# A gated mix of two spectral filters: another division of PSUM in the loop of steps, and another order of products and gate sums

## The chip, the cores and the metric

The kernel runs on one core of one Trainium2 chip. The metric is the time of one execution on the device in microseconds (us); each time shown is the median of several runs.

## The reference

Two filters are applied to the same input `x` (2048 × 1024, bf16), each a two-dimensional real Fourier transform, a pointwise product with complex weights and the inverse transform; a gate of one number per row mixes them.

```python
def ref(x, w_r, w_i):
    X = rfft2(x.astype(float32))
    return irfft2(X * (w_r + 1j * w_i), s=(S, D)).astype(bfloat16)

g = sigmoid((x * gate_w).sum(-1, keepdims=True))
return g * ref(x, A_w_r, A_w_i) + (1 - g) * ref(x, B_w_r, B_w_i)
```

The gate's sum over a row is taken from the spectrum too, since only the forward transform of the columns is at hand when it is needed.

## The kernel before, in words

Both filters share one forward transform, and the two inverse transforms are mixed before the last stage. All transforms are matrix products with constant matrices.

- Stage 1 (`stage1`, L387) transforms along one part of the rows; `fold3` (L442, VectorE) adds and subtracts halves of the result. The parts for the first four row frequencies go to the small tiles EO and VD.
- Then comes the **loop of steps**, 16 of them, one for each pair of row frequencies in each half of the columns. `SEQ` gives the order: pairs (half 0, p = 0, 1, 2), (half 1, p = 0), (half 0, p = 3 to 7), (half 1, p = 1 to 7). In this text "pair i" is entry i of SEQ; pairs 0 to 8 without pair 3 are the first pass over half 0, and pair 8 is its last. `step(i)` issues stage 4 of pair i (`stage4`, L481; evicted from PSUM by ScalarE, L485, into one of six buffers X), the swap of real and imaginary rows of X into a buffer XS (`swap`, two DMAs, L290; on POOL's queue for i up to 7, on SP's after), and stage 2 of pair i + 2 (`stage2`, L455 and L464; evicted by ScalarE, L470, into one of three buffers CS). Behind each step come the gate's matmuls (`gate_spectrum`, L511, eight for each row frequency), whose 32 columns are evicted once (L660, into GSB) in step 10, and the products of that step.
- A **product** (`product`, L499, VectorE) multiplies X (for `sw` = 0) or XS (`sw` = 1) of a pair by the weights of both filters: (i, 0) and (i, 1) in ORDER. The entries with two more numbers are products of one half only. The weights are loaded by SP's queue in the order of p; pair 8 (p = 7) needs the last of them.
- The **groups** (`group`, L606) are the first part of the inverse transform: 16 matmuls each into a slot of two banks, evicted by ScalarE (L616) or VectorE (L614). Groups 0 to 15 need the products of half 0, groups 16 to 31 those of half 1. `spare` hands out the slots in turn: three of them until step 15 is issued, then four.
- The **gate**: `row_sums` (three instructions of VectorE, L526 to L530) makes the sums from GSB. `zsum` (L553, 32 matmuls, and a sigmoid by ScalarE, L556, into VD) and `gate_mask` (L562) make the mask for one half of the rows; `rbgen` (L593) multiplies the constant matrix by the mask, which gives 16 row blocks RB.
- Stages 6 (L735) and 7 (L760) are the rest of the inverse transform, row block by row block, with their evictions and sums (L745, L767, L743, L807, L771, and L812 on POOL) and the stores.

PSUM has eight banks. In the loop, stage 2 uses banks 0 and 1 in each step (pair 1 uses 4 and 5, pairs 13 and 15 use 6 and 7), stage 4 the banks 2 and 3 or 4 and 5 in turn, and the gate's columns lie in bank 6, after the gate weights in bank 7.

What orders the work: each engine runs its instructions in the order in which the program adds them. An instruction names keys that it reads and writes (a bank, a buffer), and the program adds semaphore waits for the earlier instructions on these keys. Nothing is reordered. Several reads and writes of VD share one key, so that a fold into VD also waits for the matmuls that read VD before.

Of the kernel before, what the change touches and what calls it, by code (L numbers as in the profile page):

```python
# [5 lines left out]
ACT = mybir.ActivationFunctionType  # L6
# [228 lines left out]
def bass_gated_mix__spectral_gfnet__spectral_gfnet__prompt_kernel(nc, A_x, A_w_r, A_w_i, B_x, B_w_r, B_w_i, gate_w, out):  # L235
# [22 lines left out]
    VD = sb("VD", 1024)  # L258
# [24 lines left out]
    P = Prog()  # L283
# [142 lines left out]
    def fblock(cmb, j, t):  # L426
        if cmb in (1, 2):
            return sl(FT, cmb * 4096 + j * 2048 + t * 128, [(1, 128)])
        if t < 4:
            return sl((EO, VD)[t // 2], cmb // 3 * 512 + j * 256 + t % 2 * 128, [(1, 128)])  # L430
        return sl(FT, cmb * 4096 + j * 2048 + (t - 4) * 128, [(1, 128)])

    def ekeys(i, cs, s):
        return [("E", i, cs, s)] + ["VD"] * (i == 1)
# [10 lines left out]

    def stage2(i, css=(0, 1), ab=(0, 1)):
        hf, p = SEQ[i]
        b0 = 4 if i == 1 else 6 if i in (13, 15) else 0
        if 0 in ab:
            for cs in css:  # L450
                for t in (2 * p, 2 * p + 1):
                    for j in range(2):
                        o = ps((b0 + t % 2) * 512 + cs * 256 + 32, [(96, 2), (64, 2), (1, 32)])
                        rh = sl(F2, 256 + 512 * cs + 256 * j + hf * 128, [(1, 128)])
                        P.add("pe", lambda e, o=o, cs=cs, j=j, t=t, rh=rh: e.matmul(o, fblock(1 + cs, j, t), rh, start=(j == 0), stop=(j == 1)),  # L455
                              r=[("F1", cs, j), "F2"], w=[bank(b0 + t % 2)])
        if 1 in ab:
            for cs in css:
                for t in (2 * p, 2 * p + 1):
                    for w in range(2):  # L460
                        v = 1 - w if cs else w
                        o = ps((b0 + t % 2) * 512 + cs * 256 + 64 * v, [(224 - 128 * v, 2), (1, 32)])
                        rh = sl(F2, 1280 * cs + w * 128 + hf * 64, [(1, 64)])
                        op = P.add("pe", lambda e, o=o, cs=cs, t=t, w=w, rh=rh: e.matmul(o, fblock(3 * cs, w, t), rh, start=True, stop=True),  # L464
                                   r=ekeys(p, cs, w) + ["F2"], w=[bank(b0 + t % 2)])
        if css == (0,) or ab == (0,):
            return
        dst, src = sl(XF, CSo(i), [(1, 1024)]), ps(b0 * 512, [(128, 8), (1, 32), (32, 4)])
        kw = dict(r=[bank(b0), bank(b0 + 1)], w=[("CS", i % 3)], after=last1)
        P.add("act", lambda e: e.activation(dst, src, ACT.Copy), **kw)  # L470
        return op

    def stage4(i):
        b0 = 2 + 2 * (i % 2 if i < STEP5 else 0)
        parts = [(1, 0, 1), (0, 1, 1)] if SEQ[i][1] == 0 else [(0, 0, 2)]
        for pm in range(2):
            for kind, q, n in parts:
                for m in range(2):
                    o = ps((b0 + pm) * 512 + q * 256, [(1, n * 256)])
                    rh = sl(XF, CSo(i) + 512 * q + 256 * m, [(512, n), (1, 256)])  # L480
                    P.add("pe", lambda e, o=o, kind=kind, pm=pm, m=m, rh=rh: e.matmul(o, sl(CK, fbo(kind, pm, m), [(1, 128)]), rh,  # L481
                                                                                      start=(m == 0), stop=(m == 1)),
                          r=[("CS", i % 3), "CK"], w=[bank(b0 + pm)])
        dst = sl(XF, Xo(i), [(1, 1024)])
        P.add("act", lambda e: e.activation(dst, ps(b0 * 512, [(256, 2), (512, 2), (1, 256)]), ACT.Copy), r=[bank(b0), bank(b0 + 1)],  # L485
              w=[("X", i % NX)], after=last1)

    def swap(i):
        eng = ("pool", "sp")[i > 7]
        for ri in range(2):  # L490
            dma(eng, f"xs{i}", sl(MM, XSo(i), [(1, 1024)], p0=1 - ri, np_=64, pstep=2), sl(XF, Xo(i), [(1, 1024)], p0=ri, np_=64, pstep=2),
                r=[("X", i % NX)], **({"a": [("XS", i % NX)]} if ri else {"w": [("XS", i % NX)]}), after=last1)
# [15 lines left out]

    def gate_spectrum(t):
        for m in range(8):  # L510
            P.add("pe", lambda e, m=m: e.matmul(ps(6 * 512 + 2 * t, [(1, 2)]), fblock(m // 2, m % 2, t), sl(CK, GWo + 2 * m, [(1, 2)]),  # L511
                                                start=(m == 0), stop=(m == 7)), r=["GW2"] + ([("F1", m // 4, m % 2)] if m // 2 in (1, 2) else ekeys(t // 2, m // 4, m % 2)), w=[bank(6)])

    def star_column(b):
        for o, n, kind, pm, off in ((2, 15, 0, 0, 3), (3, 15, 0, 1, 3), (0, 1, 1, 0, 1), (1, 1, 1, 1, 1)):
# [32 lines left out]

    GMo = lambda r: (XF, 7168 + r * 256) if r < 8 else (MM, 4096 + (r - 8) * 256)

    def zsum(u, hf):
        for n in range(32):
            P.add("pe", lambda e, n=n: e.matmul(ps(u * 1024 + 32 * n, [(1, 32)]), sl(AB, n, [(0, 128)]), sl(CL, MKo + 32 * hf, [(1, 32)]),  # L553
                                                start=True, stop=True),
                  r=["AB", "CV"], w=[bank(2 * u + n // 16)])
        P.add("act", lambda e: e.activation(sl(VD, 0, [(1, 1024)]), ps(u * 1024, [(1, 32), (32, 32)]), ACT.Sigmoid, scale=SM[:, 0:1]),  # L556
              r=[bank(2 * u), bank(2 * u + 1), "SM"], w=["VD"])

    def gate_mask(hf):
        t, o = GMo(8 * hf)  # L560
        for h in range(2):
            P.add("dve", lambda e, h=h: e.tensor_scalar(  # L562
                out=sl(t, o + h * 32, [(64, 32), (1, 32)]), in0=sl(VD, 0, [(32, 32), (1, 32)]),
                scalar1=SM[:, 1 + h:2 + h], scalar2=None, op0=ALU.mult),
                r=["VD", "SM"], w=[("GM", hf, h), ("XS" if hf else "X", 4), ("XS" if hf else "X", 5)])


    def col0(u, sw):
# [51 lines left out]
    for cs in range(2):  # L620
        for i in range(2):
            fold3(i, (cs,))
        for ab in range(2):
            for i in range(2):
                stage2(i, (cs,), (ab,))
            if cs == ab == 0:
                gate_weights(7)
    for i in range(2, 6):
        fold3(i)
    load("CL", CL, 576, CL.shape[1] - 576, cst["CL"].ap()[:, 576:], w=["CL", "GR", "GRr"])  # L630
# [4 lines left out]
    def step(i):  # L635
# [5 lines left out]
        if i == 15:  # L641
            dma("sp", "U5", sl(FT, U5o, [(2048, 8), (1, 1024)]).bitcast(u16), cst["U5"].ap().rearrange("p (a b) -> p a b", a=8), w=["U5"], after=[last2])


    ORDER = (((0, 0),), ((1, 0),), ((2, 0),), ((3, 0),), ((0, 1), (4, 0)), ((1, 1), (2, 1), (5, 0)), ((3, 1), (6, 0)), ((4, 1), (7, 0)),
             ((5, 1), (8, 0, 0, 1)), ((6, 1), (7, 1)), ((8, 1, 0, 1), (8, 0, 1, 1), (8, 1, 1, 1), (9, 0)), ((9, 1), (10, 0)), ((10, 1), (11, 0)), ((11, 1), (12, 0)))

    def products(i):
        for a in ORDER[i]:
# [3 lines left out]
    for i in range(STEP5):  # L653
        step(i)
        for _ in range(2 if i == 0 else 1):
            if gt < 16:
                gate_spectrum(gt)
                gt += 1
        if i == 10:
            P.add("act", lambda e: e.activation(GSB[:], ps(6 * 512, [(1, 32)]), ACT.Copy), r=[bank(6)], w=["GSB"])  # L660
        if i in (1, 9):
            save512(i // 8, 0)
        products(i)
        if i in (1, 9):
            save512(i // 8, 1)
        if i < 2:
            fold3(6 + i)
        if i == 12:
            row_sums()


    slots = [2, 3, 0]
# [1 line left out]
    def spare():  # L674
        slots.append(slots.pop(0))
        return slots[-1]
# [3 lines left out]
    def groups(n):  # L680
        for _ in range(n):
            group(spare(), todo.pop(0), "act")
# [11 lines left out]
    groups(8)  # L694
    for a in ((13, 1), (14, 1), (15, 0, 0, 1), (15, 1, 0, 1), (15, 0, 1, 1), (15, 1, 1, 1)):
        product(*a)
    zsum(spare(), 0)
    gate_mask(0)
    for k, name in enumerate(("DI", "DJ")):
        dma("sp", name, sl(FT, DIo + k * 4096, [(2048, 2), (1, 1024)]).bitcast(u16), cst[name].ap().rearrange("p (a b) -> p a b", a=2), w=[name], after=[last2])  # L700
    groups(3)
# [1 line left out]
    for sw in range(2):  # L703
        col0(u, sw)
    groups(3)
    for n, g in enumerate(range(16, 32)):
        if n == 3:
            zsum(spare(), 1)
        group(spare(), g, "dve" if n % 4 == 2 else "act")
        if n == 5:  # L710
            gate_mask(1)
        if n < 14:
            rbgen(n, "dve")
    rbgen(14, "dve")
    rbgen(15, "dve")
    last5 = P.ops["pe"][-1]


# [103 lines left out]
    outs, late = [], []  # L822
    stage6(0)
    stage6(1)
    for r in range(16):
        if 0 < r < 14:
            stage6(r + 2)
        late += stage7(r)
        if r < 13:
            outs.append(late.pop()())  # L830
        if r == 0:
            stage6(2)
# [63 lines left out]
```

## Time and profile before

| | |
|---|---|
| median of 3 runs | 126.29 us (126.19 to 127.03) |
| profiled execution, time | 126.23 us |
| profiled execution, span | 124.3 us |
| busy share of the span: PE / DVE / ACT / POOL | 93% / 81% / 80% / 31% |
| PE, ACT, DVE busy from 30 to 48 us (18 us) | 17.2, 18.0, 15.3 |
| PE, ACT, DVE busy from 53 to 68 us (15 us) | 15.0, 15.0, 14.9 |
| TensorE clock granted, mean | 0.995 of full speed |

The busy times come from one execution, recorded by the profiler; times inside it count from the start of the span. PE is TensorE, ACT is ScalarE, DVE is VectorE, SP and POOL are the two that mostly issue DMAs here. A row of the timeline has the start, the duration, the engine, the line of the kernel, the operation with what it writes and reads, how many instructions are merged, and in brackets the idle time before it with what ended it. A row of the chain has the start, the time and what the chain passed through; "issue" is time in which nothing that the profile shows was waited for. A matmul's record is longer than the distance to the next one, since matmuls overlap.

### The profile page before, as it was taken

The page shows a single profiled execution, that of the slowest core. Times are in us where ns is not written, and L with a number is a line of the kernel's source. Part 1 is how long each engine was busy: PE and PEld are TensorE (multiplying, and loading weights), DVE is VectorE, ACT ScalarE, POOL GpSimd, SP SyncE. Part 2 cuts the span into 40 slices and gives each one's busy share as a digit, 9 for nine tenths or more (in the row PEclk, how much of TensorE's full clock was granted, in tenths as well). Part 3 has the DMA queues.
Part 4 walks back from the last instruction along what each step waited for, and adds up shares of the span by engine and source line. Part 5 has one row for each costly group of instructions (what it writes and reads, how often), then busy time and mean ns, then how long its engine had stood idle before and what let it go on. Part 6 is the DMA issues. An engine that isn't in the chain of part 4 may idle for free.

```text
span 124.3 us, 3754 instructions
## 1 busy us (share of the span) xinstructions
PE 116.1 (93%) x1588; PEld 96.6 (78%) x1588; DVE 100.9 (81%) x169; ACT 100.0 (80%) x117; POOL 38.6 (31%) x45
## 2 busy tenths in 40 slices
PE   6998999799999999999999999999799999999960
PEld 4676688676565655679999999999799989898730
DVE  0568999789795996999999989999835778777890
ACT  4249896699999999999999997779579868688620
POOL 1000051006546300000000000000008999999990
PEclk9999999999999999999999999999999999999998
DMA  2999999999999999432699300000000233425356
GB/s 85 316 409 432 405 342 356 350 350 357 330 377 358 367 363 343 156 129 93 174 403 390 140 0 5 0 5 0 0 5 0 84 126 133 169 86 202 142 187 235
DMA packets 17600, 26.11 MB, mean 210 GB/s; under 512 B 2096, under 2 KB 11056, under 8 KB 17456
## 3 DMA queue, kind: packets, MB, share of 16 engines
q1 hardware_dynamic: 16384, 23.26, 53.3%
q0 software_dynamic: 768, 2.10, 4.6%
q10 hardware_dynamic: 432, 0.52, 1.4%
q8 instruction: 12, 0.20, 0.7%
q14 instruction: 4, 0.03, 0.1%
HBM read 17.48 MB, written 4.19 MB: 174 GB/s over the span
## 4 chain that ended last, share of the span: by engine, by line
PE 73%; ACT 11%; DMA 6%; DVE 4%; issue 2%; SPq 2%; DVEq 0%
PE PS L606 25%; PE PS L760 13%; PE PS L735 12%; ACT XF L470 8%; PE PS L387 7%; PE PS L455 6%; DMA WB<-in_A_x_dram 6%; PE PS L481 4%; PE PS L464 3%; DVE XF L348 2%; SPq L290 2%; DVE WA L771 1%; PE PS L553 1%; ACT FT L396 1%; ACT XF L485 1%
## 5 line engine op out<-in xcount | busy, mean ns | idle before, releaser
L812 POOL TENSOR_TENSOR WA<-WA 128x512 bf16<-128x512 f32 x22 | 27.3, 1275 | 51.6 <-DVE WA L807 51.4
L606 PE MATMUL PS<-CL,WB 128*128 128x128 bf16 x256 | 31.9, 226 | 0.0
L606 PE MATMUL PS<-CL,WA 128*128 128x128 bf16 x256 | 31.7, 223 | 0.0
L606 PEld LDWEIGHTS PS<-CL,WB 128*128 128x128 bf16 x256 | 31.3, 145 | 0.6 <-DVE WA L499 0.4
L606 PEld LDWEIGHTS PS<-CL,WA 128*128 128x128 bf16 x256 | 31.4, 145 | 0.1
L616 ACT ACTIVATE WB<-PS 128x1024 bf16<-128x1024 f32 (+1 forms) x29 | 27.6, 1020 | 2.3 <-PE PS L606 2.2
L499 DVE TENSOR_TENSOR WB<-XF,WA 128x2048 bf16<-128x2048 bf16 (+1 forms) x18 | 20.0, 1110 | 3.6 <-DMA WA<-in_B_w_i_dram 2.1
L745 ACT ACTIVATE WA<-PS 128x1024 bf16<-128x1024 f32 (+1 forms) x16 | 15.8, 996 | 6.7 <-PE PS L735 6.7
L499 DVE TENSOR_TENSOR WA<-MM,WA 128x2048 bf16<-128x2048 bf16 (+1 forms) x18 | 19.8, 1111 | 0.6 <-DMA MM<-XF 0.6
L807 DVE TENSOR_TENSOR WA<-PS,WA 128x512 f32<-128x512 f32 x22 | 14.2, 686 | 6.7 <-ACT WA L767 4.2
L760 PE MATMUL PS<-FT,WA 128*128 128x256 bf16 (+1 forms) x132 | 19.3, 292 | 0.0
L470 ACT ACTIVATE XF<-PS 128x1024 bf16<-128x1024 f32 x16 | 16.3, 1025 | 0.7 <-PE PS L464 0.6
L485 ACT ACTIVATE XF<-PS 128x1024 bf16<-128x1024 f32 x16 | 16.5, 1034 | 0.3 <-PE PS L481 0.2
L387 PE MATMUL PS<-MM,XF 128*128 128x256 bf16 x128 | 16.2, 284 | 0.5 <-DVE XF L348 0.3
L481 PE MATMUL PS<-XF,CK 128*128 128x512 bf16 (+1 forms) x72 | 16.4, 355 | 0.0
L387 PEld LDWEIGHTS PS<-MM,XF 128*128 128x128 bf16 x128 | 12.6, 101 | 4.2 <-DVE XF L348 2.2
L760 PEld LDWEIGHTS PS<-FT,WA 128*128 128x128 bf16 x132 | 12.3, 98 | 3.2
L396 ACT ACTIVATE FT<-PS 128x1024 bf16<-128x1024 f32 x13 | 12.4, 1028 | 2.2 <-PE PS L387 2.2
L290 POOL DMA_DIRECT2D MM<-XF x16 | 8.8, 551 | 14.7 <-PE PS L481 8.7
L455 PEld LDWEIGHTS PS<-F,FT 128*128 128x128 bf16 x128 | 7.5, 98 | 7.0 <-ACT XF L470 5.6
L455 PE MATMUL PS<-F,FT 128*128 128x128 bf16 x128 | 10.0, 220 | 1.1 <-ACT GSB L660 0.2
L348 DVE TENSOR_TENSOR XF<-WB 128x512 bf16<-128x512 bf16 (+1 forms) x20 | 6.0, 365 | 6.2 <-DMA WB<-in_A_x_dram 6.2
(76 smaller groups left out, 137.8 us busy)
## 6 DMA issues: line engine op xcount, KB each, us to landing
out_dram<-WA SPq DMA_DIRECT2D x14, 256.0 KB, 2.2
MM<-XF POOLq DMA_DIRECT2D x16, 128.0 KB, 5.2
MM<-XF SPq DMA_DIRECT2D x16, 128.0 KB, 2.7
FT<-c_U SPq DMA_DIRECT2D x1, 2048.0 KB, 9.7
WB<-in_A_x_dram SPq DMA_DIRECT2D x3, 512.0 KB, 6.1
WA<-in_A_w_r_dram SPq DMA_DIRECT2D x4, 256.5 KB, 5.7
WA<-in_A_w_i_dram SPq DMA_DIRECT2D x4, 256.5 KB, 5.8
WA<-in_B_w_r_dram SPq DMA_DIRECT2D x4, 256.5 KB, 5.7
```

The lines of the kernel that those rows point to most:

```text
L387: P.add("pe", lambda e, o=o, lh=lh, rh=rh, s=s: e.matmul(o, lh, rh, start=(s == 0), stop=(s == 1)), r=[("xf", c % 2, q, h, s ^ j), ("M", c ...
L455: P.add("pe", lambda e, o=o, cs=cs, j=j, t=t, rh=rh: e.matmul(o, fblock(1 + cs, j, t), rh, start=(j == 0), stop=(j == 1)), r=[("F1", cs, j ...
L470: P.add("act", lambda e: e.activation(dst, src, ACT.Copy), **kw)
L481: P.add("pe", lambda e, o=o, kind=kind, pm=pm, m=m, rh=rh: e.matmul(o, sl(CK, fbo(kind, pm, m), [(1, 128)]), rh, start=(m == 0), stop=(m = ...
L485: P.add("act", lambda e: e.activation(dst, ps(b0 * 512, [(256, 2), (512, 2), (1, 256)]), ACT.Copy), r=[bank(b0), bank(b0 + 1)], w=[("X", i ...
L499: P.add("dve", lambda e: e.tensor_tensor(out=at(sw), in0=sl(xt, xo + 64 * h0, [(0, 2), (128, 8), (1, 64 * n)]), in1=at(1), op=ALU.mult), r ...
L606: P.add("pe", lambda e, o=o, l0=l0, ab=ab: e.matmul(o, sl(WT[ab], l0, [(RWS[ab] // 2, 128)]), sl(CL, KIo[ab], [(1, 128)]), start=(ab == 0) ...
L616: P.add("act", lambda e, s=src, d=dst: e.activation(d, s, ACT.Copy), r=b, a=["Z"])
L735: P.add("pe", lambda e, o=o, lh=lh, rh=rh, cp=cp: e.matmul(o, lh, rh, start=(cp == 0), stop=(cp == 1)), r=["Z", ("RB", r)], w=[bank(b0 + b ...
L745: P.add("act", lambda e, s=src, d=dst: e.activation(d, s, ACT.Copy), **kw)
L760: P.add("pe", lambda e: e.matmul(ps(col, [(1, n * 256)]), lh, rh, start=(k == 0), stop=(k == last)), r=[("Y", r), "DI"] + ["DJ"] * (full o ...
L812: P.add("pool", lambda e, s=s, op=op: e.tensor_tensor(out=ods(s, 0, 2), in0=pv[:, :, 0, :], in1=pv[:, :, 1, :], op=op), r=[("PQ", pk, 0), ...
```

## The change

- Stage 2 of pair i uses banks 0 and 1 for even i, 6 and 7 for odd i, throughout.
- Stage 4 of step i uses banks 2 and 3 for even i, 3 and 4 for odd i, so bank 3 is common to both; the matmuls of the bank that isn't shared with the step before come first. Steps 14 and 15 use banks 2 and 3.
- The gate's columns lie in bank 5, the gate weights in bank 4.
- Swap 8 goes to POOL's queue.
- `ORDER` changes: all products of pairs 0 to 7 come before those of pair 8.
- `row_sums` moves from step 12 to a place behind the last products. The first `zsum`, which stood between the groups of half 0 and half 1, moves behind group 18; the second one moves from before group 19 to behind it, and writes EO in place of VD.
- Of groups 16 to 31 VectorE evicts 16 and 18 (before: 18, 22 and 26), and still a half each of 30 and 31. The `rbgen` calls start after group 20, two of them in two places, and the last two come behind stage 6 of row blocks 0 and 1.

```diff
 def stage2(i, css=(0, 1), ab=(0, 1)):
     hf, p = SEQ[i]
-    b0 = 4 if i == 1 else 6 if i in (13, 15) else 0
+    b0 = 6 * (i % 2)
...
 def stage4(i):
-    b0 = 2 + 2 * (i % 2 if i < STEP5 else 0)
+    bk = ((2, 3), (3, 4))[i % 2 if i < STEP5 else 0]
     parts = [(1, 0, 1), (0, 1, 1)] if SEQ[i][1] == 0 else [(0, 0, 2)]
-    for pm in range(2):
+    for pm in (0, 1) if bk[0] == 2 else (1, 0):
         for kind, q, n in parts:
             for m in range(2):
-                o = ps((b0 + pm) * 512 + q * 256, [(1, n * 256)])
+                o = ps(bk[pm] * 512 + q * 256, [(1, n * 256)])
...
-    eng = ("pool", "sp")[i > 7]
+    eng = ("pool", "sp")[i > 8]
...
-                gate_weights(7)
+                gate_weights(4)
...
-ORDER = (((0, 0),), ((1, 0),), ((2, 0),), ((3, 0),), ((0, 1), (4, 0)), ((1, 1), (2, 1), (5, 0)), ((3, 1), (6, 0)), ((4, 1), (7, 0)),
-         ((5, 1), (8, 0, 0, 1)), ((6, 1), (7, 1)), ((8, 1, 0, 1), (8, 0, 1, 1), (8, 1, 1, 1), (9, 0)), ((9, 1), (10, 0)), ((10, 1), (11, 0)), ((11, 1), (12, 0)))
+ORDER = (((0, 0),), ((1, 0),), ((2, 0),), ((3, 0),), ((0, 1), (4, 0)), ((1, 1), (2, 1)), ((3, 1), (5, 0)), ((6, 0), (4, 1), (5, 1)),
+         ((7, 0), (6, 1), (7, 1)), ((8, 0, 0, 1), (8, 1, 0, 1), (8, 0, 1, 1)), ((8, 1, 1, 1), (9, 0)), ((9, 1), (10, 0)), ((10, 1), (11, 0)),
+         ((11, 1), (12, 0)))
...
-        if i == 12:
-            row_sums()
...
 for a in ((13, 1), (14, 1), (15, 0, 0, 1), (15, 1, 0, 1), (15, 0, 1, 1), (15, 1, 1, 1)):
     product(*a)
-zsum(spare(), 0)
-gate_mask(0)
+row_sums()
...
+rb = list(range(16))
 for n, g in enumerate(range(16, 32)):
-    if n == 3:
-        zsum(spare(), 1)
-    group(spare(), g, "dve" if n % 4 == 2 else "act")
-    if n == 5:
-        gate_mask(1)
-    if n < 14:
-        rbgen(n, "dve")
-rbgen(14, "dve")
-rbgen(15, "dve")
+    group(spare(), g, "dve" if n in (0, 2) else "act")
+    if n in (2, 3):
+        zsum(spare(), n - 2)
+    if n in (3, 5):
+        gate_mask(n // 2 - 1)
+    for _ in range((n > 3) + (n in (9, 12))):
+        rbgen(rb.pop(0), "dve")
...
 stage6(0)
 stage6(1)
+for r in rb:
+    rbgen(r, "dve")
```

More of the change, by code (lines that the diff above doesn't have):

```diff
@@ L482, in stage4 @@
                                                                                       start=(m == 0), stop=(m == 1)),
[L483 to L486, printed above, removed]
+                          r=[("CS", i % 3), "CK"], w=[bank(bk[pm])])
+        dst, src = sl(XF, Xo(i), [(1, 1024)]), ps(bk[0] * 512, [(256, 2), (512, 2), (1, 256)])
+        P.add("act", lambda e: e.activation(dst, src, ACT.Copy), r=[bank(k) for k in bk], w=[("X", i % NX)], after=last1)
     def swap(i):
-        eng = ("pool", "sp")[i > 7]
+        eng = ("pool", "sp")[i > 8]
         for ri in range(2):
@@ L510, in gate_spectrum @@
         for m in range(8):
-            P.add("pe", lambda e, m=m: e.matmul(ps(6 * 512 + 2 * t, [(1, 2)]), fblock(m // 2, m % 2, t), sl(CK, GWo + 2 * m, [(1, 2)]),
-                                                start=(m == 0), stop=(m == 7)), r=["GW2"] + ([("F1", m // 4, m % 2)] if m // 2 in (1, 2) else ekeys(t // 2, m // 4, m % 2)), w=[bank(6)])
+            P.add("pe", lambda e, m=m: e.matmul(ps(5 * 512 + 2 * t, [(1, 2)]), fblock(m // 2, m % 2, t), sl(CK, GWo + 2 * m, [(1, 2)]),
+                                                start=(m == 0), stop=(m == 7)), r=["GW2"] + ([("F1", m // 4, m % 2)] if m // 2 in (1, 2) else ekeys(t // 2, m // 4, m % 2)), w=[bank(5)])
     def star_column(b):
@@ L549, in bass_gated_mix__spectral_gfnet__spectral_gfnet__prompt_kernel @@
     GMo = lambda r: (XF, 7168 + r * 256) if r < 8 else (MM, 4096 + (r - 8) * 256)
+    Zs = (VD, EO)
     def zsum(u, hf):
@@ L555, in zsum @@
                   r=["AB", "CV"], w=[bank(2 * u + n // 16)])
-        P.add("act", lambda e: e.activation(sl(VD, 0, [(1, 1024)]), ps(u * 1024, [(1, 32), (32, 32)]), ACT.Sigmoid, scale=SM[:, 0:1]),
-              r=[bank(2 * u), bank(2 * u + 1), "SM"], w=["VD"])
+        P.add("act", lambda e: e.activation(sl(Zs[hf], 0, [(1, 1024)]), ps(u * 1024, [(1, 32), (32, 32)]), ACT.Sigmoid, scale=SM[:, 0:1]),
+              r=[bank(2 * u), bank(2 * u + 1), "SM"], w=[("VD", "EO")[hf]] + [("E", 0, cs, s) for cs in range(2) for s in range(2)] * hf)
     def gate_mask(hf):
@@ L562, in gate_mask @@
             P.add("dve", lambda e, h=h: e.tensor_scalar(
-                out=sl(t, o + h * 32, [(64, 32), (1, 32)]), in0=sl(VD, 0, [(32, 32), (1, 32)]),
+                out=sl(t, o + h * 32, [(64, 32), (1, 32)]), in0=sl(Zs[hf], 0, [(32, 32), (1, 32)]),
                 scalar1=SM[:, 1 + h:2 + h], scalar2=None, op0=ALU.mult),
-                r=["VD", "SM"], w=[("GM", hf, h), ("XS" if hf else "X", 4), ("XS" if hf else "X", 5)])
+                r=[("VD", "EO")[hf], "SM"], w=[("GM", hf, h), ("XS" if hf else "X", 4), ("XS" if hf else "X", 5)])
     def col0(u, sw):
@@ L659, in bass_gated_mix__spectral_gfnet__spectral_gfnet__prompt_kernel @@
         if i == 10:
-            P.add("act", lambda e: e.activation(GSB[:], ps(6 * 512, [(1, 32)]), ACT.Copy), r=[bank(6)], w=["GSB"])
+            P.add("act", lambda e: e.activation(GSB[:], ps(5 * 512, [(1, 32)]), ACT.Copy), r=[bank(5)], w=["GSB"])
         if i in (1, 9):
```

## The prediction, made before the changed kernel was run

> **What bounds the kernel now.** I read the page first, for its span; then the chain of waits; then the timelines of ScalarE (ACT), TensorE (PE) and VectorE (DVE) around the places that the diff touches.
>
> ```profile
> span 124.3 us, 3754 instructions
> ```
>
> The profiled execution took 126.23 us, so 1.93 lie outside this span; the median of the three runs is 126.29, 0.06 above it. The sum is made against 126.23 and the 0.06 is added at the end. The chain in order of time (start, duration, what):
>
> ```profile
> 29.03 1.03 ACT XF L470
> 30.06 0.05 issue
> 30.11 0.62 PE PS L455 x8
> 30.73 0.29 PE PS L464 x8
> 31.02 0.02 issue
> 31.04 1.03 ACT XF L470
> ...
> 68.56 5.87 PE PS L606 x96
> 74.44 0.79 PE PS L553 x32
> 75.23 12.72 PE PS L606 x208
> ...
> 87.97 0.61 ACT WB L616
> ```
>
> Two regimes are to be seen. In the loop of steps the chain goes in a circle: ACT empties stage 2's slot (L470, 1.03), then PE may fill the same two banks again (0.05 + 0.62 + 0.29 + 0.02), then ACT empties them again: 31.04 − 29.03 = 2.01 us a step. Stage 2 has one slot there, so eviction and refill never overlap. Later PE runs without a pause (208 matmuls of L606 in 12.72 us, 0.978 a group of 16) until the last eviction at 87.97. So what the change does in the loop counts as far as it moves the start of that PE run; what it does inside the run counts only if it makes PE wait.
>
> The loop, by the timeline of ACT alone (start, duration):
>
> ```profile
> 28.05 1.02 ACT L485 ACTIVATE XF<-PS 128x1024 bf16<-128x1024 f32 x1
> ...
> 48.04 0.19 ACT L660 ACTIVATE GSB<-PS 128x32 bf16<-128x32 f32 x1
> 48.14 1.02 ACT L485 ACTIVATE XF<-PS 128x1024 bf16<-128x1024 f32 x1
> 49.22 1.02 ACT L470 ACTIVATE XF<-PS 128x1024 bf16<-128x1024 f32 x1
> ...
> 51.95 1.04 ACT L485 ACTIVATE XF<-PS 128x1024 bf16<-128x1024 f32 x1
> ...
> 54.66 1.08 ACT L616 ACTIVATE WB<-PS 128x1024 bf16<-128x1024 f32 x1
> ```
>
> L485 at 28.05 is step 1, at 51.95 step 13. From 49.22 on the kernel already has a second slot (steps 13 and 15 use banks 6 and 7), and there ACT runs back to back: six evictions later, at 54.66, the next one starts. By starts that is 5.44 / 6 = 0.907; by ends (50.24 to 55.74, since the durations grow) 5.50 / 6 = 0.917. I take 0.917, the rate at which they finish: two evictions a step make 1.834, against 2.01.
>
> PE by its timeline:
>
> ```profile
> 28.79 0.34 PE L511 MATMUL PS<-CK,FT 128*128 128x2 bf16 x8
> 29.00 1.02 PE L481 MATMUL PS<-XF,CK 128*128 128x512 bf16 x4
> ...
> 49.84 0.61 PE L455 MATMUL PS<-F,FT 128*128 128x128 bf16 x8
> 50.29 0.40 PE L464 MATMUL PS<-F,FT 128*128 128x64 bf16 x8
> 50.52 1.03 PE L481 MATMUL PS<-XF,CK 128*128 128x512 bf16 x4
> 51.38 0.61 PE L455 MATMUL PS<-F,FT 128*128 128x128 bf16 x8
> ...
> 53.13 0.25 PE L606 MATMUL PS<-CL,WB 128*128 128x128 bf16 x1
> ```
>
> From start to start, unhindered: stage 2 takes 0.45 + 0.23, stage 4 0.86 (51.38 − 50.52), the gate's eight matmuls 0.21: 1.75 a step. Below ACT's 1.834, but closely.
>
> **The parts of the change.**
>
> *Two slots of stage 2.* The refill no longer waits for the eviction just begun, so ACT sets the loop. From the end of L485 of step 1 (29.07) to that of step 13 (52.99) are 23.92 us now. After: 12 × 1.834 plus 0.10 for L660 (48.14 − 48.04) = 22.11. Gain 1.81. By starts, 0.907, it would be 2.05.
>
> *Three banks of stage 4.* Banks (2, 3) and (3, 4) in turn share bank 3, so the second half of each stage 4 (two matmuls, 0.43) waits for L485 of the step before. After that end: wake-up 0.05 (the chain's row at 30.06), 0.43 of issue, 0.17 until the last matmul is through (1.03 − 0.86), 0.02, then L485 itself, 1.02: a circle of 1.69, less than 1.834, so no cost. Behind the waiting half, on PE's queue, stand stage 2, the gate's matmuls and the first half of the next stage 4: PE's circle is the 1.75, hidden with 0.08 to spare. ACT's L470 behind this is done with two evictions in hand.
>
> *The first stage 2 of step 1.* It moves from banks 4 and 5 to 6 and 7, the slot that stage 1's last eviction frees last; the gate weights go to bank 4. So four matmuls of L455 that ran before that eviction's end now come after it, ahead of the reads of VD, for which VectorE's next fold waits.
>
> ```profile
> 23.05 0.28 PE L464 MATMUL PS<-F,VD 128*128 128x64 bf16 x4
> 23.16 0.61 PE L455 MATMUL PS<-F,FT 128*128 128x128 bf16 x8
> 23.61 0.28 PE L464 MATMUL PS<-F,EO 128*128 128x64 bf16 x4
> ```
>
> Eight of L455 take 0.45, four 0.22. The gate weights' matmul, which waited for that eviction too, came 0.14 after it, a plain wake-up is 0.05; the 0.09 between them may be hidden behind the four. Cost 0.13 to 0.22; I take 0.15, nearer the lower end, since the four themselves need only the plain wake-up.
>
> *The end of the loop.* The first group (L606) needs bank 4, which L485 of step 13 empties: now 53.13 − 52.99 = 0.14 after it. After: the second half of step 14's stage 4 first waits for that same eviction (bank 3), so 0.05 + 0.43, with 0.02 for the next issue, 0.50. Cost 0.36; 0.34 without the 0.02, 0.45 if the group's longer wake-up (0.14, not 0.05) is what any first matmul there pays.
>
> *Products and row sums.* These are DVE's, off the path; the question is whether they stay off, since PE now starts earlier.
>
> ```profile
> 38.37 1.24 DVE L499 TENSOR_TENSOR WA<-MM,WA 128x2048 bf16<-128x2048 bf16 x1 [0.57 <-DMA MM<-XF]
> ...
> 48.89 0.70 DVE L499 TENSOR_TENSOR WB<-XF,WA 128x1024 bf16<-128x1024 bf16 x1 [1.20 <-DMA WA<-in_B_w_i_dram]
> ...
> 59.59 0.68 DVE L526 TENSOR_TENSOR VD<-CL,GSB 128x512 f32<-128x512 bf16 x1
> ...
> 61.11 1.24 DVE L499 TENSOR_TENSOR WA<-MM,WA 128x2048 bf16<-128x2048 bf16 x1
> 62.26 1.23 DVE L499 TENSOR_TENSOR WB<-XF,WA 128x2048 bf16<-128x2048 bf16 x1
> ...
> 69.93 0.70 DVE L499 TENSOR_TENSOR WA<-MM,WA 128x1024 bf16<-128x1024 bf16 x1
> ```
>
> First bound, the first group. DVE now starts pair 8 at 48.89, when its weights land, with (6,1) and (7,1) still to do. After, pairs 0 to 7 all go before pair 8. The wait at 38.37 is for swap 2 and stays (L485 of step 2 would start near 30.04, now 30.06); nine products follow, each 62.26 − 61.11 = 1.15: 48.7, or 49.4 if 0.7 more of swap waits appear. Then two half products (0.70 by the record, 0.6 apart) and a copy that is short beside them: 50.2 if only the weights hold it, 50.8 from 49.4. The group wants them at about 53.13 − 1.30 = 51.8. Second bound, the second pass (groups 16 on): PE reaches it now at 68.56 + 3 × 0.978 = 71.5; after, at 71.5 − 1.3 − 0.79 = 69.4, since the first gate sum (32 matmuls of L553) comes later. DVE ends the halves that it needs at 69.93 + 0.70 = 70.6. After, row sums go behind (61.11 − 59.59 = 1.52 off), two products were done in what was waiting time (2.3 off), and pair 8 starts up to 0.5 later: 67.3. So these parts gain nothing by themselves; without them DVE, at 70.6, would hold PE 1.2 from 69.4 on.
>
> *Swap 8 on POOL's queue.* POOL is idle there, SP has the last weights to issue. Its 0.26 MB now move beside the weights and not behind them.
>
> ```profile
> DMA packets 3998, 5.34 MB, mean 356 GB/s; under 512 B 588, under 2 KB 3130, under 8 KB 3995
> ```
>
> At 356 GB/s that is 0.74 us, by which the last weights may land later (48.89 becomes 49.63) if the two queues share alike. The Trainium skill, "DMA: Bandwidth & Descriptors", section "Queues, rings and completion order", says that each DMA engine takes turns, packet by packet, between the queues that have work, which would make it the 0.74. Then pair 8's half products end near 51.0, still before 51.8: no cost, but 0.8 of cover left.
>
> *The second pass on ACT and the last rows.*
>
> ```profile
> 75.27 1.11 ACT L556 ACTIVATE VD<-PS,SM 128x1024 bf16<-128x1024 f32 x1 [0.74 <-PE PS L553]
> ```
> ```profile
> 86.05 0.68 DVE L593 TENSOR_TENSOR MM<-FT,MM 128x1024 bf16<-128x1024 bf16 x1
> 86.66 0.68 DVE L614 CAST WB<-PS 128x512 bf16<-128x512 f32 x1
> 87.49 0.69 DVE L614 CAST WB<-PS 128x512 bf16<-128x512 f32 x1 [0.16 <-PE PS L606]
> ...
> 92.30 1.29 DVE L807 TENSOR_TENSOR WA<-PS,WA 128x512 f32<-128x512 f32 x2 [1.87 <-ACT WA L767]
> ```
>
> From the end of the first gate sum to the last whole group, ACT has two sigmoids (1.11) and eleven evictions (0.917): 12.3. PE needs 11 × 0.978 + 0.79 = 11.5, and an eviction ends about 1.1 behind its group anyway: 12.6, so ACT keeps up. Of the row blocks (L593), one now stands between DVE's two last half evictions: it takes 0.61 (86.66 − 86.05), so the second would start at 86.66 + 1.22 = 87.88 instead of 87.49 and end at 88.57, level with ACT's own last half (87.97 + 0.61 = 88.58). Cost 0 to 0.1; I take 0.03. The two blocks moved behind stage 6 take 1.2 and fall into the 1.87 that DVE idles before 92.30. Behind that the code is the same.
>
> **Sum.** −1.81 + 0.15 + 0.36 + 0.03 = −1.27; 126.23 − 1.27 = 124.96, and with the 0.06, 125.0. By the bounds: −2.05 + 0.13 + 0.34 = −1.58 (124.7), and −1.81 + 0.22 + 0.45 + 0.10 = −1.04 (125.25).
>
> **The rivals.**
>
> *ACT is full already.* Each eviction's record is 1.02 long, and two of them fill a step of 2.01. If an eviction really occupied ACT for 1.02, twelve steps would last 24.5 and nothing would be gained. The 0.917 from 49.22 on speaks against it, but the sample is of seven, in steps without the gate's matmuls. Between them, with 0.95 each, the loop lasts 12 × 1.90 + 0.10 = 22.9: −1.02 + 0.54 = −0.5, 125.8. The Trainium skill, "ScalarE: Activation LUTs", section "What ACT_TABLE_LOAD costs", gives 186 ns + 0.833 ns an element for such an instruction and an overlap of about 93 ns back to back: an estimate from that page of 0.946 for 1024 elements, by which the sum would be this rival's. The trace's 0.917 decides for me. Chance 0.08.
>
> *The shared bank binds.* PE's circle of 1.75 has 0.08 of cover. If stage 4's two halves each pay a wake-up of 0.05 that I don't count in it, a step is 1.85, and with the longer one of 0.14 for one of them 1.94; at 1.88, 12 × 0.046 = 0.55 is lost: −0.7, 125.6. For it: the margin is thin. Against it: when PE comes late, the eviction is done and there is nothing to wake up for. Chance 0.11.
>
> *The products become the bound, and the end is slower.* The first group waits for pair 8 on both of DVE's inputs, and now everything of DVE stands ahead of pair 8, while swap 8 travels on POOL's queue beside the last weights. Each us by which (8,1) ends behind 51.8 is a us on the path; from 1.3 behind, 53.1, the kernel is slower than before.
>
> ```profile
> MM<-XF POOLq DMA_DIRECT2D x16, 128.0 KB, 5.2
> ```
>
> Swap 8 is sent when L485 of step 8 ends, 28.05 + 0.15 + 7 × 1.834 + 1.02 = 42.1, and with 5.2 lands near 47.3, or 48.4 by its second half. If it, or the weights, come 1.5 us later than the 51.0 above allows, 0.7 is on the path: 125.7. If 3.4 later, 2.6 are: 127.6. For it: DVE did wait for swaps and weights in this loop (the rows of 38.37 and 48.89). Against it: 0.8 of cover. Chance 0.09, of which 0.06 as slow as the second, 0.03 as the first.
>
> **How the numbers follow.** My own case has 0.72. A measurement of this kernel can tell about 1% from no change: below 125.03 is faster, above 127.55 slower. My case lies across that line, 124.7 to 125.25, and somewhat more of it below than above, as the errors that I can name go a little further down (0.27, most of it the 0.907 by starts) than up: 0.45 faster, 0.27 the same. With the rivals (0.08, 0.11 and 0.03 the same, 0.06 slower): faster 0.45, the same 0.49, slower 0.06. The range reaches from the lower bound with a little more, 124.5, to the rivals at 125.7 and 125.8: 124.5 to 125.9, which leaves out the slower cases and the ends of mine.
>
> **What would show it.** Right: in the loop, L470 and L485 start 0.91 to 0.92 apart and a step takes about 1.83; PE's wait for L485 stands in the middle of L481, not before L455; the first product of the loop comes about 0.15 later; L606 begins near 51.8, about 0.5 after the end of step 13's L485; the last L616 starts 1.2 to 1.3 earlier than 87.97. Wrong: steps of 1.9 or more; a wait of the first L606 for DVE, with L499 waiting for DMA just before it; waits of L606 around groups 16 to 20 for DVE or ACT; a last half eviction by DVE that ends behind ACT's.

## The result, and the profile after

| | before | after |
|---|---|---|
| median, runs side by side | 126.19 us (6 runs) | 124.84 us (6 runs) |
| ratio, with its 95% interval | | 0.9891 (0.9851 to 0.9931) |
| profiled execution, time and span | 126.23, 124.3 | 124.56, 122.5 |

The kernel is 1.1% faster; the interval reaches from 0.7% to 1.5%. Of the 1.67 us between the two profiled executions some is no work of the change: the input arrives earlier in the second one, so that everything before the loop lies 0.37 earlier. I therefore count from a fixed point below, the start of ScalarE's last two evictions of stage 1.

```profile
20.80 1.94 ACT L396 ACTIVATE FT<-PS 128x1024 bf16<-128x1024 f32 x2 [0.72 <-PE PS L387]
```

and in the profile after

```profile
20.43 1.94 ACT L396 ACTIVATE FT<-PS 128x1024 bf16<-128x1024 f32 x2 [0.72 <-PE PS L387]
...
27.83 1.02 ACT L485 ACTIVATE XF<-PS 128x1024 bf16<-128x1024 f32 x1
28.75 1.02 ACT L470 ACTIVATE XF<-PS 128x1024 bf16<-128x1024 f32 x1
...
35.07 1.11 ACT L485 ACTIVATE XF<-PS 128x1024 bf16<-128x1024 f32 x1
...
36.88 1.14 ACT L485 ACTIVATE XF<-PS 128x1024 bf16<-128x1024 f32 x1
37.80 1.13 ACT L470 ACTIVATE XF<-PS 128x1024 bf16<-128x1024 f32 x1
38.72 1.14 ACT L485 ACTIVATE XF<-PS 128x1024 bf16<-128x1024 f32 x1
...
45.14 1.13 ACT L470 ACTIVATE XF<-PS 128x1024 bf16<-128x1024 f32 x1
...
49.81 1.14 ACT L485 ACTIVATE XF<-PS 128x1024 bf16<-128x1024 f32 x1
```

These rows are ACT's timeline (start, duration). A step is now 38.72 − 36.88 = 1.84 instead of 2.01, and from there on each eviction's record begins 0.2 before the one before it has ended: its input was there, ACT was the one that was late. The ends stand evenly apart, 0.916 (29.77 to 36.18, seven evictions) and 0.917 (38.02 to 46.27, nine). From the end of L485 of step 1 (28.85) to that of step 13 (50.95) are 22.10 us, where there were 23.92.

What PE waits for has changed place. The view of waits, sums over the kernel:

```profile
PEld PS L481 <- ACT XF L485: 5.6, 13, 0.7
```

These are thirteen waits of the weight loads (PEld) in the middle of stage 4, for the bank that it shares with the step before, 0.43 each on average; the waits of L455 for L470 (5.6 us before, ten times) are gone. The loads run ahead of the matmuls, so the matmuls themselves pause for less: stage 4 takes 38.52 − 37.57 = 0.95 from start to start, where 0.86 is unhindered.

```profile
37.57 1.11 PE L481 MATMUL PS<-XF,CK 128*128 128x512 bf16 x4
38.52 0.61 PE L455 MATMUL PS<-F,FT 128*128 128x128 bf16 x8
```

And the end of the loop, in PE's timeline:

```profile
50.28 1.32 PE L481 MATMUL PS<-XF,CK 128*128 128x512 bf16 x4
51.44 0.22 PE L607 MATMUL PS<-CL,WB 128*128 128x128 bf16 x1
```

The four matmuls of step 14's stage 4 last 1.32 instead of 1.03 because the second pair waits for L485 of step 13; the first group (L606 before, L607 now) starts 0.49 behind that eviction's end. From there PE runs without a pause, as before:

```profile
74.50 11.71 PE PS L607 x192
86.21 0.02 issue
86.23 0.60 ACT WB L617
```

That is the chain of waits; from the first group to the last eviction it is 34.79 us, before 34.84. The chain now names PE, not ACT, for the loop (PE 81% of the span, ACT 4%; before 73% and 11%). That is no contradiction to the rows of ACT: PE's circle and ACT's are nearly equal, and the wait of 0.09 within the four merged matmuls is counted as PE's.

### The profile page after: what moved, and what is told of

It reads as the page before. It is cut to its first block, busy times and chain, and to the rows that moved or that the text cites. A ratio compares the mean times of both kernels' runs of the same rounds, so it can differ in the third digit from the quotient of the medians.

```text
span 122.5 us, 3751 instructions
## 1 busy us (share of the span) xinstructions
PE 114.7 (94%) x1588; PEld 96.3 (79%) x1588; DVE 100.1 (82%) x168; ACT 99.3 (81%) x118; POOL 39.8 (33%) x47
## 4 chain that ended last, share of the span: by engine, by line
PE 81%; DMA 5%; DVE 4%; ACT 4%; SPq 2%; issue 1%; DVEq 0%
PE PS L607 26%; PE PS L758 13%; PE PS L733 12%; PE PS L481 11%; PE PS L387 7%; DMA WB<-in_A_x_dram 5%; PE PS L455 5%; PE PS L464 3%; PE PS L510 2%; DVE XF L348 2%; ACT XF L485 2%; SPq L290 2%; DVE WA L769 1%; PE PS L554 1%; ACT XF L470 1%
## 5 line engine op out<-in xcount | busy, mean ns | idle before, releaser
L607 PE MATMUL PS<-CL,WB 128*128 128x128 bf16 x256 | 31.9, 226 | 0.0
L607 PE MATMUL PS<-CL,WA 128*128 128x128 bf16 x256 | 31.7, 223 | 0.0
L607 PEld LDWEIGHTS PS<-CL,WB 128*128 128x128 bf16 x256 | 31.3, 145 | 0.2
L607 PEld LDWEIGHTS PS<-CL,WA 128*128 128x128 bf16 x256 | 31.3, 145 | 0.1
L617 ACT ACTIVATE WB<-PS 128x1024 bf16<-128x1024 f32 (+1 forms) x30 | 28.7, 998 | 1.4 <-PE PS L607 1.3
L481 PE MATMUL PS<-XF,CK 128*128 128x512 bf16 (+1 forms) x72 | 17.7, 357 | 0.4 <-ACT XF L485 0.2
L470 ACT ACTIVATE XF<-PS 128x1024 bf16<-128x1024 f32 x16 | 17.4, 1096 | 0.6 <-PE PS L464 0.6
L485 ACT ACTIVATE XF<-PS 128x1024 bf16<-128x1024 f32 x16 | 17.5, 1096 | 0.2 <-PE PS L481 0.2
L387 PE MATMUL PS<-MM,XF 128*128 128x256 bf16 x128 | 15.7, 280 | 0.4 <-DVE XF L348 0.2
L290 POOL DMA_DIRECT2D MM<-XF x18 | 9.9, 551 | 14.6 <-PE PS L481 8.9
L455 PEld LDWEIGHTS PS<-F,FT 128*128 128x128 bf16 x128 | 8.4, 98 | 4.0 <-ACT FT L396 1.1
L455 PE MATMUL PS<-F,FT 128*128 128x128 bf16 x128 | 9.9, 220 | 0.9 <-ACT FT L396 0.9
```

The lines of the kernel that those rows point to most:

```text
L387: P.add("pe", lambda e, o=o, lh=lh, rh=rh, s=s: e.matmul(o, lh, rh, start=(s == 0), stop=(s == 1)), r=[("xf", c % 2, q, h, s ^ j), ("M", c ...
L485: P.add("act", lambda e: e.activation(dst, src, ACT.Copy), r=[bank(k) for k in bk], w=[("X", i % NX)], after=last1)
L607: P.add("pe", lambda e, o=o, l0=l0, ab=ab: e.matmul(o, sl(WT[ab], l0, [(RWS[ab] // 2, 128)]), sl(CL, KIo[ab], [(1, 128)]), start=(ab == 0) ...
L617: P.add("act", lambda e, s=src, d=dst: e.activation(d, s, ACT.Copy), r=b, a=["Z"])
```

## The experiments

All ratios are to the kernel before, from runs side by side, with 95% intervals; its median was 126.13 to 126.39 in the three further sets of runs. The last two columns are from each profile: the start of the first group with both its inputs there, and its distance from the start of stage 1's last two evictions.

| kernel | median | ratio | first group | distance |
|---|---|---|---|---|
| before | 126.19 | 1 | 53.13 | 32.33 |
| after | 124.84 | 0.9891 (0.9851 to 0.9931) | 51.44 | 31.01 |
| PSUM alone | 125.49 | 0.9949 (0.9915 to 0.9983) | 52.39 | 31.62 |
| all but PSUM | 126.30 | 1.0007 (0.9990 to 1.0024) | 53.16 | 32.33 |
| after, one slot of stage 2 | 126.64 | 1.0043 (1.0008 to 1.0078) | 53.48 | 32.68 |
| after, stage 4 on two banks | 129.27 | 1.0266 (1.0205 to 1.0327) | 57.42 | 36.67 |
| after, old order of products | 126.34 | 0.9996 (0.9973 to 1.0020) | 53.46 | 32.49 |
| after, swap 8 on SP | 124.89 | 0.9904 (0.9867 to 0.9941) | 51.80 | 31.01 |
| after, row sums early | 124.86 | 0.9905 (0.9872 to 0.9937) | 51.61 | 31.01 |
| after, stage 1's slots turned | 124.44 | 0.9857 (0.9826 to 0.9888) | 51.27 | 30.55 |
| after, step 13 on banks 4 and 5 | 124.54 | 0.9852 (0.9823 to 0.9881) | 51.38 | 30.66 |
| both of these | 124.15 | 0.9832 (0.9805 to 0.9859) | 50.91 | 30.20 |

**The division of PSUM alone**, on the kernel before:

```diff
-    b0 = 4 if i == 1 else 6 if i in (13, 15) else 0
+    b0 = 6 * (i % 2)
...
-    b0 = 2 + 2 * (i % 2 if i < STEP5 else 0)
+    bk = ((2, 3), (3, 4))[i % 2 if i < STEP5 else 0]
```

(with the order of stage 4's halves, the gate in bank 5 and its weights in bank 4, as in the change)

> The kernel before with the new division of PSUM alone; products, row sums, gate sums, swap 8 and row blocks as before. My theory: the loop's steps become 1.83 us, but the first group then waits for VectorE, whose order still has (6,1) and (7,1) behind the wait for pair 8's weights: (8,1) ended at 52.73 us in the profile of before and stays there, so the first L606 starts at 52.8 in place of 53.13 and the time is about 0.3 us below the kernel before, ratio 0.997. The rival, that the products are never on the path and the division of PSUM alone carries the gain: ratio 0.989 as for the whole change.

About half of the gain: 0.9949. The loop has the short steps (L485 at 37.22 and 39.06 in its profile), but PE then stands before the first group:

```profile
51.78 0.22 PE L605 MATMUL PS<-CL,WB 128*128 128x128 bf16 x1
52.39 0.27 PE L605 MATMUL PS<-CL,WA 128*128 128x128 bf16 x1 [0.39 <-DVE WA L498]
```

The group's first matmul reads the products with sw = 0 and starts; the second reads those with sw = 1 and waits for VectorE. So neither theory's number was met exactly, but the mechanism is mine: what is lost against the whole change, 31.62 − 31.01 = 0.61, is this wait. It is less than the 1.0 that I expected because in this profile the weights land earlier than in the one of before (pair 8 starts 27.72 after the fixed point, 28.09 before). From the first group to the last eviction this kernel takes 34.82 and the whole change 34.79, so the moved gate sums and row blocks show no gain beyond 0.03 between these two; no run took them singly.

**Everything but the division of PSUM**, the changed kernel with the places above taken back:

> The change without the new division of PSUM: all products of pairs 0 to 7 ahead of pair 8, row sums behind the products, gate sums behind groups 18 and 19, swap 8 on POOL, on the banks of before. My theory: VectorE was not on the path, so nothing is gained: ratio 0.998 to 1.002, steps still 2.01 us, the first L606 near 53.1. The rival, that the new place of products, row sums and gate sums carries part of the gain by itself: ratio below 0.996.

No gain, 1.0007, and the first group stands at the same distance as before, 32.33. Together, the order of the products, the row sums, the gate sums and swap 8 are worth nothing without the shorter loop.

**One slot of stage 2:**

```diff
-    b0 = 6 * (i % 2)
+    b0 = 6 if i in (1, 13, 15) else 0
```

> The changed kernel with stage 2 in one slot again (banks 0 and 1; 6 and 7 only for pairs 1, 13 and 15), everything else as changed. My theory: steps of 2.01 us come back, 10 of the steps are 0.18 longer: 1.8 us above the changed kernel, and, as the wait for the shared bank at the end of the loop stays, slightly above the kernel before: ratio to before 1.00 to 1.004. The rival, that the shared bank or ScalarE alone sets the step and the second slot does nothing: ratio 0.989.

As expected, 1.0043: slower than before. ACT's timeline has the old step (37.22 to 39.23):

```profile
37.22 1.02 ACT L470 ACTIVATE XF<-PS 128x1024 bf16<-128x1024 f32 x1
38.24 1.02 ACT L485 ACTIVATE XF<-PS 128x1024 bf16<-128x1024 f32 x1
39.23 1.02 ACT L470 ACTIVATE XF<-PS 128x1024 bf16<-128x1024 f32 x1
```

The second slot carries the gain (32.68 − 31.01 = 1.67). The 0.35 by which this kernel stands behind the one before is a net figure: it pays 0.15 at the start of the loop (step 1's L485 is 7.40 after the fixed point, 7.25 before) and 0.36 at its end (the first group 0.50 behind L485 of step 13, 0.14 before), and gains 0.16 within the loop (23.76 in place of 23.92). That 0.16 is at one place: before, the gate's columns lay in bank 6, and the first stage 2 that uses it, pair 13's, waited for their eviction:

```profile
48.29 0.62 PE L455 MATMUL PS<-F,FT 128*128 128x128 bf16 x8 [0.18 <-ACT GSB L660]
```

With the columns in bank 5 this wait is gone. So of the 1.82 that the loop gains by the whole change, 1.66 come from the second slot.

**Stage 4 on two banks:**

```diff
-    bk = ((2, 3), (3, 4))[i % 2 if i < STEP5 else 0]
+    bk = (2, 3)
```

> The changed kernel with stage 4 of every step on banks 2 and 3, no third bank. My theory of the circle: wake-up 0.05, the whole of stage 4 0.86, 0.17 until its last matmul is through, 0.02 and L485 of 1.02 are 2.12 us a step in place of 1.83, so some 3.4 us more over twelve steps and 0.4 more at the end of the loop: about 128.4 to 128.7, ratio to before 1.018 to 1.020. The rival, that ScalarE's rate hides this too (only half of the wait is new): 1.9 us a step at most, 125.6, ratio 0.995.

The circle binds, and a little harder than I reckoned: 1.0266.

```profile
36.08 1.02 ACT L485 ACTIVATE XF<-PS 128x1024 bf16<-128x1024 f32 x1 [0.22 <-PE PS L481]
37.00 1.02 ACT L470 ACTIVATE XF<-PS 128x1024 bf16<-128x1024 f32 x1
38.24 1.02 ACT L485 ACTIVATE XF<-PS 128x1024 bf16<-128x1024 f32 x1 [0.22 <-PE PS L481]
```

A step is 2.15 (38.24 − 36.08 = 2.16; 25.85 us over twelve steps), against 2.12 reckoned and 1.83 in the changed kernel. ACT now waits for PE in each step. Twelve steps are 3.87 longer (25.85 − 21.98 between the starts of L485 of steps 1 and 13), and the first group starts 1.96 behind the start of the last of them instead of 1.63: 4.2 together, and the medians are 129.27 − 124.84 = 4.4 apart. The place of its first group in the table isn't used: the clock of TensorE was lower for a moment in this profile (last section).

**The old order of products:**

```diff
-ORDER = (... ((1, 1), (2, 1)), ((3, 1), (5, 0)), ((6, 0), (4, 1), (5, 1)), ((7, 0), (6, 1), (7, 1)), ...
+ORDER = (... ((1, 1), (2, 1), (5, 0)), ((3, 1), (6, 0)), ((4, 1), (7, 0)), ((5, 1), (8, 0, 0, 1)), ((6, 1), (7, 1)), ...
```

> The changed kernel with the old ORDER of products alone; row sums stay behind the products. My theory: the first L606 waits for (8,1), which ends near 52.4 to 52.7 instead of 50.97, so the time is 1.0 to 1.3 us above the changed kernel, ratio to before 0.997 to 1.000. The rival, that only the row sums' place mattered: ratio 0.989.

The whole gain is gone, 0.9996, and PE's timeline has the reason in one row:

```profile
51.98 0.22 PE L607 MATMUL PS<-CL,WB 128*128 128x128 bf16 x1
53.46 0.27 PE L607 MATMUL PS<-CL,WA 128*128 128x128 bf16 x1 [1.26 <-DVE WA L498]
```

The loss is not the order's alone. PSUM alone has the old order too and still gains 0.5%. Ahead of the first group the two kernels differ in the queue of swap 8 only, on POOL here and on SP there: pair 8 starts 28.59 after the fixed point here (49.56 − 20.97) and 27.72 there, 0.87 apart, and so are the first groups (32.49 and 31.62); the medians are 0.85 apart (ratios 0.9996 and 0.9949). So the 1.48 by which this kernel stands behind the changed one is 0.61 with swap 8 on SP's queue, and 0.87 more with it on POOL's.

**Row sums early:**

```diff
+        if i == 12:
+            row_sums()
...
-    row_sums()
```

> The changed kernel with the row sums back in step 12, everything else as changed. My theory: VectorE's products end 1.5 us later, so the halves for the second pass at about 69.0 in place of 67.46, just when PE comes to group 16 (68.94): a cost of 0 to 0.2 us, ratio to before 0.989 to 0.991. The rival, that the row sums' place was worth what they last: 1.5 us, ratio 1.001.

No difference from the changed kernel (0.9905 and 0.9891, the same distance of 31.01). The three instructions cost VectorE 1.5 us, but even so it has the halves for the second pass at 68.74 (68.04 + 0.70), and PE comes to group 16 near 69.1 (the row of the chain below, and three of its six groups).

```profile
66.17 5.88 PE PS L607 x96
```

**Swap 8 on SP's queue:**

```diff
-    eng = ("pool", "sp")[i > 8]
+    eng = ("pool", "sp")[i > 7]
```

> The changed kernel with swap 8 on SP's queue again, behind the last weights. My theory: the swap lands before VectorE comes to (8,1) at 50.3 either way, so nothing changes: ratio 0.987 to 0.991. The rival, that swap 8 on SP's queue comes too late for (8,1): up to 1 us more, ratio 0.997. The other one, that on POOL's queue it delays the last weights and with them the save and pair 8: up to 0.5 us less, ratio 0.985.

No difference either. But one rival is seen at work, below the surface: on SP's queue the swap is late, and (8,1) waits for it.

```profile
50.39 0.70 DVE L498 TENSOR_TENSOR WA<-MM,WA 128x1024 bf16<-128x1024 bf16 x1 [0.46 <-DMA MM<-XF]
```

Whether the weights are late with the swap on POOL's queue is less clear. The last weights' DMA is issued, and VectorE's wait for it ends, in the profile of PSUM alone (swap 8 on SP) at

```profile
42.45 0.61 SPq L290 DMA_DIRECT2D WA<-in_B_w_i_dram  x1
...
48.49 0.70 DVE L498 TENSOR_TENSOR WB<-XF,WA 128x1024 bf16<-128x1024 bf16 x1 [1.23 <-DMA WA<-in_B_w_i_dram]
```

and in that of the old order (swap 8 on POOL) at

```profile
42.73 0.61 SPq L290 DMA_DIRECT2D WA<-in_B_w_i_dram  x1
...
49.56 0.70 DVE L498 TENSOR_TENSOR WB<-XF,WA 128x1024 bf16<-128x1024 bf16 x1 [1.36 <-DMA WA<-in_B_w_i_dram]
```

6.04 from issue to use in the one, 6.83 in the other; 6.02 in the kernel before (48.89 − 42.87) and 6.85 with the row sums early (49.28 − 42.43). That would be 0.8 for the swap, where 0.74 was estimated. But the pair that differs in nothing else doesn't bear it out: from issue to landing the last weights took 6.9 in the profile with swap 8 on SP and 6.7 in that of the changed kernel. There they land 1.1 later, counted from the fixed point (29.05 and 27.97), but they were also issued 1.3 later (22.35 and 21.07), and the B_w_i weights before them, issued ahead of swap 8, 1.4 later already (19.73 and 18.36). So what the swap costs the weights is shown in the kernels with the old order, where pair 8 waits for them (0.87, above), and stays open in those with the new order; there neither delay arrives on the path.

**Two costs of the change, taken away.** First the shared bank at the end of the loop:

```diff
-    bk = ((2, 3), (3, 4))[i % 2 if i < STEP5 else 0]
+    bk = (4, 5) if i == 13 else ((2, 3), (3, 4))[i % 2 if i < STEP5 else 0]
```

> The changed kernel with stage 4 of step 13 on banks 4 and 5 (bank 5 is free once the gate's columns are evicted in step 10), so that step 14's stage 4 shares no bank with it. It measures the 0.36 that the prediction put on the shared bank at the end of the loop. My theory: PE's wait for L485 of step 13 falls only on the first group, which starts 0.14 after that eviction's end and not 0.5: the first L606 0.3 earlier, 0.25 to 0.35 us below the changed kernel, ratio to before 0.986. (8,1) ends at 50.97, which leaves just this much. The rival, that the products hold the first group at the same place: no gain, ratio 0.989.

```profile
50.38 1.04 PE L481 MATMUL PS<-XF,CK 128*128 128x512 bf16 x4
51.38 0.25 PE L607 MATMUL PS<-CL,WB 128*128 128x128 bf16 x1
```

L485 of step 13 ends at 51.24 there (50.09 + 1.15); the group starts 0.14 after it, 0.35 earlier than in the changed kernel, and the median is 0.30 lower. Second, the start of the loop:

```diff
-    cnt = 0
+    cnt = 2
```

(`cnt` is the slot with which stage 1 begins.)

> The changed kernel with stage 1's four PSUM slots taken in another turn (the first product of stage 1 starts in slot 2 in place of slot 0), so that stage 1's last eviction frees banks 2 and 3, which nobody waits for; the first stage 2 of pairs 0 and 1 and the gate weights' matmul no longer wait for it. It tests the 0.15 that the prediction put on the start of the loop. My theory: the four matmuls, the gate weights and the reads of VD move ahead of that eviction's end, VectorE's fold into VD follows the fold into EO at once, and L481 of step 0 starts 0.3 to 0.4 us earlier, counted from stage 1's last two evictions; the loop moves with it, but the first group then waits for (8,1), whose end is set by weights and swaps: 0.2 to 0.4 below the changed kernel, ratio to before 0.986 to 0.988. The rival, that the fold waits for stage 1's data anyway: no gain, ratio 0.989.

```profile
20.72 1.94 ACT L396 ACTIVATE FT<-PS 128x1024 bf16<-128x1024 f32 x2 [0.72 <-PE PS L387]
...
25.71 1.02 ACT L485 ACTIVATE XF<-PS 128x1024 bf16<-128x1024 f32 x1 [0.22 <-PE PS L481]
```

Step 0's L485 starts 4.99 after the fixed point instead of 5.46 (25.89 − 20.43): 0.47 earlier, a little more than expected, and all of it arrives at the first group (31.01 − 30.55 = 0.46). The intervals of these two kernels overlap that of the changed kernel, so the gain of each rests on its profile. Last, both together:

> The changed kernel with both: stage 1's slots in the other turn, and stage 4 of step 13 on banks 4 and 5. If the two costs were independent, their gains would add up: 0.35 and 0.35, 124.2, ratio to before 0.983. My theory: in the profile of the version with step 13 on banks 4 and 5, (8,1) ends about 0.8 before the first group, so most of the second gain is still to be had, but weights and swaps, which don't move, take up to 0.3 of it: 124.2 to 124.5, ratio 0.983 to 0.985. The rival, that the products hold the first group: no gain over one of the two alone, ratio 0.985 to 0.987.

The gains add up (31.01 − 30.20 = 0.81), 124.15 us. It is the fastest version of this study, 1.7% below the kernel before; its interval only touches that of the changed kernel, and the 0.7 between the medians agrees with the 0.8 in the profile. (8,1) ends at 50.73 in it (50.03 + 0.70) and the group starts at 50.91: the products are next now, as the last theory had it, but they don't hold it yet.

## Why the prediction was right

The forecast was 125.0 and the result 124.84. Term by term, from the profiles and counted from the fixed point:

| term | forecast | measured |
|---|---|---|
| loop, ends of L485 from step 1 to step 13 | −1.81 (22.11 us) | −1.82 (22.10 us) |
| start of the loop (step 0's L485: 5.31 before, 5.46 after) | +0.15 | +0.15 |
| end of the loop (first group behind L485: 0.14 before, 0.49 after) | +0.36 | +0.35 |
| from the first group to the last eviction (34.84, 34.79) | +0.03 | −0.05 |
| sum | −1.27 | −1.37 |

The medians differ by 1.35.

**The pace of ACT.** The 0.917 between ends was right and the 0.907 between starts would have been wrong by 0.24: the records grow from 1.02 to 1.14 and then stay there, while the ends keep their distance of 0.917. The growth stops where the input comes just in time: stage 4 in the row at 37.57 ends at 38.68, and its eviction's record begins 0.04 later, at 38.72. It is no limit of ACT's own: with step 13 on banks 4 and 5, where the stage 4 behind it needn't wait, the records grow on, to 1.23 at L485 of step 15. The first rival would have had the loop at 22.9. By the Trainium skill, "ScalarE: Activation LUTs", section "What ACT_TABLE_LOAD costs", whose figures give 0.946 as an estimate, it would be 22.8; the trace has 22.10, so here the measurement decides.

**The shared bank** doesn't bind within the loop, as the sum said: the weight loads wait 0.43 in each step and the matmuls 0.09, and ACT is late all the same. The margin is thin. The circle through the shared half has about 0.12 to spare, an estimate from the records: the eviction's is 1.14 long there, and 1.02 when its predecessor is done. What happens without the margin the kernel with two banks shows: the same circle with a whole stage 4 in it makes 2.15. The reckoned 2.12 was 0.03 short.

**The products as a rival** were real, and their cover smaller than I had it. (8,1) ends at 50.97 in the profile after:

```profile
32.55 1.23 DVE L498 TENSOR_TENSOR WB<-XF,WA 128x2048 bf16<-128x2048 bf16 x1 [0.46 <-ACT XF L485]
...
37.95 2.62 DVE L498 TENSOR_TENSOR WA<-MM,WA 128x2048 bf16<-128x2048 bf16 x2 [0.63 <-DMA MM<-XF]
41.18 2.38 DVE L498 TENSOR_TENSOR WB<-XF,WA 128x2048 bf16<-128x2048 bf16 x2 [0.61 <-DMA WA<-in_B_w_i_dram]
...
50.28 0.69 DVE L498 TENSOR_TENSOR WA<-MM,WA 128x1024 bf16<-128x1024 bf16 x1
```

That is 0.47 ahead of the group, where I had 0.8. VectorE waits for a swap and for the weights of pair 5, and from 41.18 on is busy to the end of pair 8; I had counted 0.7 for such waits and, with the weights late by 0.74, an end of (8,1) near 51.0; in the times of the profile before it is 51.34 (50.97 + 0.37).

**That DVE would hold PE without the new places** of products and row sums was right for the order of products and wrong for the row sums. I had put both into one sentence with one price, 1.2 at the second pass. Taken apart, the old order costs 0.61 at the first group (PSUM alone), and 1.48 with swap 8 on POOL's queue (32.49 − 31.01); the early row sums cost nothing. That step was wrong: it priced the second bound, the second pass, which the order alone meets, and gave no price for the first one, the first group, where the old order is paid for.

**DVE's last half eviction** ended before ACT's (86.23 + 0.60 = 86.83), so the 0.03 was not needed:

```profile
85.98 0.69 DVE L615 CAST WB<-PS 128x512 bf16<-128x512 f32 x1
```

The chances were 0.45 for faster by over 1% and 0.49 for less, with the forecast on the line between them; the measurement, 1.1% with an interval on both sides of 1%, is as near to that line as the forecast was. The mechanism was the forecast one, term by term. What the number owes to luck is the cover of the products: taken for 0.8, it was 0.47, and weights or swaps later by more than that would have been on the path.

## What to carry to other kernels

When an engine and its buffer take turns, a second buffer is worth what the engine's pace back to back leaves of the step, and that pace is read from the ends of records that follow each other without a wait, not from their length. If PSUM has room for one bank and not for two, sharing one bank between neighbours can be enough. Here the half that doesn't share it was issued first; the other order wasn't run. Whether it is enough, the circle through the shared half says before anything is run. A gain in a loop arrives only if whatever waits at its end is ready earlier too: here half of it was lost with the old order of products, all of it with swap 8 moved as well, and everything but the division of PSUM gained nothing by itself.

## What the runs showed of the hardware that was not expected

The granted clock of TensorE fell for some 3 us in the profile of the kernel with two banks. Windows of it (stretch, length, busy time of PE, PEld, DVE, ACT and POOL, then the clock):

```profile
20.00:25.00 5.00, 3.98 (x81) 3.54 (x78) 3.97 (x13) 3.10 (x6) 0.00 (x0) 1.00 1.10 356
25.00:28.00 3.00, 3.00 (x31) 2.45 (x28) 1.70 (x6) 2.01 (x3) 0.00 (x0) 0.55 1.10 349
```

At 0.55 the eight matmuls of step 0's stage 4 took 1.78 instead of 1.05, and this one execution lasted 130.56, 1.3 above the kernel's median. What set it off the runs don't show.

The name behind an idle time can be wrong where a wait has several semaphores. Before the first group, the profile of the kernel before and that of step 13 on banks 4 and 5 both put 0.4 of the idle time of PE's weight loads down to VectorE, though the products that the group reads were ready at 52.73 (52.04 + 0.69) and 50.47 (49.77 + 0.70), well ahead of 53.13 and 51.38; the distance of 0.14 to the end of L485 is the same in both and points to the real one. With VectorE really late, as in the old order, the wait stands before the group's second matmul.
